# Finer waits at three seams of a spectral and dense layer stack: the returned components by quarters, the last tile's rows by halves of tokens, three late stores from another queue

One core of a Trainium2 chip. The metric is the device time of one execution in microseconds (us), lower is better.

## The reference

A stack of four residual layers on `x` of 1 x 2048 tokens x 1024 channels, bf16: spectral layer A, dense layer B, A again, B again.

```python
def _A_ref(x, w_r, w_i):                     # S = 2048 tokens, D = 1024
    X = jnp.fft.rfft2(x.astype(jnp.float32), axes=(-2, -1))
    X = X * (w_r + 1j * w_i)
    return jnp.fft.irfft2(X, s=(S, D), axes=(-2, -1)).astype(jnp.bfloat16)

def _B_ref(x, w1, b1, w2):                   # F = 3584
    h = jnp.einsum("bsd,df->bsf", x, w1) + b1
    sp = jnp.log1p(jnp.exp(-jnp.abs(h))) + jnp.where(h > 0, h, 0)
    return jnp.einsum("bsf,fd->bsd", h * jnp.tanh(sp), w2)

x = x + _A_ref(_layernorm(x), w_r, w_i)
x = x + _B_ref(_layernorm(x), w1, b1, w2)
x = x + _A_ref(_layernorm(x), w_r, w_i)
x = x + _B_ref(_layernorm(x), w1, b1, w2)
```

## The kernel before

The Fourier transforms are products with tables on TensorE. Layer A works in 8 groups `g` of 16 components. Near its end each group's tile `u` is written to DRAM and read back with components on the partitions (the "turn"), into one tile `UT`; the last products (`i4`) read it, four groups of 32 products over `l` (called dl, 0 to 127), and VectorE adds each group to `x`. From layer B to the next layer A the normalised tokens must change layout too: tile `j` (128 tokens) goes to DRAM and back into `XR`, and the last tile, 15, is copied inside SBUF row by row (`xr_direct`). A `Res` is what waits are made of: `reads` waits for its writers, `parts` writes a part of it without waiting for the other writers. Cuts are marked.

```python
    def xn_store(self, j, b):
        b.unread = False
        self.dma(self.pool, self.xn_d[j], b.ap, "xw" + b.res.name[2:], reads=[b.res], writes=[self.r_xnd[j]])

    def open_xr(self):
        self.XR = self.alloc("XR", self.o["XR"], [P, P])
        self.XR.res.begin()
        self.r_xr = [self.XR.res] * 4

    def xr_load(self, j):
        self.dma(self.pool, self.XR.ap[row_of(j, 0):row_of(j, 7) + 1:4, :, :], self.xn_d[j].rearrange(...), f"xl{j % 4}",
                 reads=[self.r_xnd[j]], parts=[self.XR.res])

    def xr_direct(self, j, b):
        for h in range(8):                            # 32 KB each, into one partition
            prog = (self.sp, self.act, self.pool)[h % 3]
            self.dma(prog, self.XR.ap[row_of(j, h):row_of(j, h) + 1, :, :], b.ap[:, h * P:(h + 1) * P], "xd" + prog.name,
                     reads=[b.res], parts=[self.XR.res])
    # ... (s1: 16 groups of 8 products, group j reads self.r_xr[j // 4])

        def u_turn(g, half):
            u = U[g % 3]
            if g == 7:                                # last group: stored in two halves of its components
                h = slice(8 * half, 8 * half + 8)
                if half == 0:
                    self.r_ud[g].begin()
                self.dma(act, self.u_d[g][:, h, :], u.ap[:, h, :], f"uwh{half}", reads=[u.res], parts=[self.r_ud[g]])
            elif half:
                self.dma(sp, self.u_d[g], u.ap, f"uw{g % 3}", reads=[u.res], writes=[self.r_ud[g]])
            if g and (half == 0) == (g == 7):
                u_back(g - 1)
            if g == 7 and half:
                u_back(7)

        def u_back(g):                                # 16 rows: g, g + 8, ...
            for i, prog in enumerate((sp, act) if g == 7 else (sp,)):
                l = slice(64 * i, 64 * i + 64) if g == 7 else slice(0, P)
                self.dma(prog, self.UT.ap[g:P:8, l, :], self.u_d[g][l].rearrange("l r n -> r l n"), f"u{prog.name}{g % 3}",
                         reads=[self.r_ud[g]], parts=[self.UT.res])
    # ... (i4: self.group(fns, reads=[self.UT.res, self.r_mt], writes=rb))
```

## Time and profile before

| | before |
|---|---|
| time | 1050.99 us median of 4 (1050.31 to 1052.5); the profiled run 1051.39, its trace spans 1049.6 |
| TensorE busy | 91% of the span |
| granted TensorE clock, mean | 0.966 |
| waits of TensorE at the three seams | 11.9, 12.0 and 11.9 us |
| DMA moved | 107 MB, 102 GB/s mean |

The three waits, 3.4% of the span, are the subject. In a wait line such as `PE PS L588 <- DMA ARENA<-ARENA: 12.0, 1, 12.0` the engine before the arrow stood for what is behind it: 12.0 us in total, once, 12.0 at most. In all views PE is TensorE, DVE VectorE, ACT ScalarE, POOL GpSimd and SP SyncE; in a DMA row each digit is the busy share of the 16 DMA engines in one slice, in tenths. Line numbers are those of each kernel's own file, so `L588` before is `L594` after, and `L901` is `L919`. The lines of before stand in the prediction.

### The profile page before, as it was taken

To read this page: it belongs to the slowest core of one execution; us is meant where nothing else is said; L and a number is where in the kernel's file an instruction comes from. 1 tells how busy PE (TensorE), PEld (TensorE's weight loads), DVE (VectorE), ACT (ScalarE), POOL (GpSimd) and SP (SyncE) were. 2 spreads that over 40 slices of the span, in tenths; PEclk is the share of its full clock that TensorE was granted. 3 is DMA by queue.
4 is the path that set the end of the run, shared out by engine and by line. 5 is a ranking of instruction groups with operands and counts; after the bars stand their busy time and mean duration, and the time that the engine had idled before them with its cause. 6 is when DMAs were issued, how large, how long until landed. Compare 5 with 4: busy or idle time off the path is not lost.

```text
span 1049.6 us, 14096 instructions
## 1 busy us (share of the span) xinstructions
PE 952.5 (91%) x5944; PEld 511.7 (49%) x6033; DVE 350.8 (33%) x776; ACT 336.5 (32%) x503; POOL 71.0 (7%) x114
## 2 busy tenths in 40 slices
PE   0799489999999999999959967999999999999998
PEld 0567465444444444444427746644444444444443
DVE  6898562531343100043326856426011100000111
ACT  6898263331000333300008844533300013340000
POOL 3242000000000000002421200000000000000000
PEclk9699789999999999999989987999999999999999
DMA  9779812464111221001941784145611112200000
GB/s 281 176 257 281 221 44 91 151 200 134 50 52 37 69 64 39 1 21 71 178 83 44 222 210 131 42 151 166 209 25 45 45 63 81 61 1 11 21 21 31
DMA packets 152718, 107.01 MB, mean 102 GB/s; under 512 B 74288, under 2 KB 131888, under 8 KB 152656
## 3 DMA queue, kind: packets, MB, share of 16 engines
q1 hardware_dynamic: 139936, 75.99, 25.4%
q0 software_dynamic: 9632, 28.45, 9.5%
q10 hardware_dynamic: 3088, 1.67, 0.6%
q8 instruction: 48, 0.79, 0.3%
q14 instruction: 14, 0.11, 0.0%
HBM read 80.85 MB, written 20.71 MB: 97 GB/s over the span
## 4 chain that ended last, share of the span: by engine, by line
PE 80%; DVE 9%; ACT 6%; DMA 3%; issue 1%; SPq 0%; ACTq 0%; DVEq 0%
PE PS L994 37%; PE PS L976 37%; DVE BN L459 2%; ACT ARENA L721 2%; PE PS L669 2%; DVE XS L915 1%; DVE ARENA L573 1%; DVE ARENA L790 1%; DMA u_scratch<-ARENA 1%; DMA ARENA<-u_scratch 1%; ACT ARENA L704 1%; DVE ARENA L951 1%; DVE ARENA L596 1%; PE PS L901 1%; ACT ARENA L792 1%
## 5 line engine op out<-in xcount | busy, mean ns | idle before, releaser
L976 PE MATMUL PS<-ARENA 128*128 128x512 bf16 (+1 forms) x1946 | 390.6, 360 | 10.3 <-DVE ARENA L951 7.2
L994 PE MATMUL PS<-ARENA 128*128 128x512 bf16 x1756 | 385.5, 379 | 1.9
L980 ACT ACTIVATE ARENA<-PS,B 128x512 bf16<-128x512 f32 (+1 forms) x248 | 159.8, 646 | 438.7 <-PE PS L976 438.7
L976 PEld LDWEIGHTS PS<-ARENA 128*128 128x128 bf16 x1984 | 194.2, 99 | 201.8 <-DVE ARENA L951 8.7
L994 PEld LDWEIGHTS PS<-ARENA 128*128 128x128 bf16 x1792 | 175.3, 98 | 211.5
L999 DVE TENSOR_TENSOR XS<-PS,XS 128x512 bf16<-128x512 f32 x64 | 44.3, 692 | 537.9 <-PE PS L994 537.9
L459 DVE BATCH_NORM_STATS2 BN<-XS 128x6 f32<-128x512 bf16 x104 | 67.2, 675 | 7.5 <-DMA XS<-in_A_x_dram 6.3
L915 DVE TENSOR_TENSOR XS<-PS,XS 128x512 bf16<-128x512 f32 (+1 forms) x40 | 29.1, 790 | 82.0 <-PE PS L901 82.0
L901 PE MATMUL PS<-MT,ARENA 128*128 128x32 bf16 (+1 forms) x768 | 24.5, 187 | 27.2 <-DMA ARENA<-u_scratch 23.8
L901 PEld LDWEIGHTS PS<-MT,ARENA 128*128 128x128 bf16 x768 | 23.0, 100 | 30.7 <-issue 24.7
L440 ACT ACTIVATE ARENA<-XS 128x1024 bf16<-128x1024 bf16 x24 | 25.3, 1055 | 36.4 <-DVE XS L915 31.5
L721 ACT ACTIVATE ARENA<-PS 128x1024 bf16<-128x1024 f32 x32 | 33.9, 1060 | 8.5 <-PE PS L717 8.5
L669 PE MATMUL PS<-FD,ARENA 128*128 128x256 bf16 (+1 forms) x256 | 33.6, 278 | 2.9 <-ACT ARENA L594 1.2
L750 ACT ACTIVATE ARENA<-PS 128x1024 bf16<-128x1024 f32 x32 | 33.9, 1061 | 3.7 <-PE PS L743 3.7
L249 POOL DMA_DIRECT2D xn_scratch<-ARENA x15 | 8.2, 550 | 390.7 <-DVE ARENA L498 390.7
L431 ACT ACTIVATE RS<-MV,EPS 128x1 f32<-128x1 f32 (+1 forms) x7 | 2.0, 292 | 98.5 <-DVE MV L462 96.2
L743 PE MATMUL PS<-ARENA 128*128 128x256 bf16 x256 | 33.2, 273 | 0.1
L743 PEld LDWEIGHTS PS<-ARENA 128*128 128x128 bf16 x256 | 24.5, 98 | 10.0 <-DVE ARENA L732 1.2
L725 DVE TENSOR_TENSOR ARENA<-ARENA 128x1024 bf16<-128x1024 bf16 x32 | 22.0, 687 | 21.9 <-ACT ARENA L721 21.9
L669 PEld LDWEIGHTS PS<-FD,ARENA 128*128 128x128 bf16 x256 | 24.5, 100 | 8.4 <-DVE ARENA L596 2.8
L764 PE MATMUL PS<-ARENA,BD 128*128 128x256 bf16 x192 | 25.9, 273 | 1.3 <-DVE ARENA L790 1.0
L498 DVE TENSOR_SCALAR ARENA<-XS,MV,RS 128x1024 bf16<-128x1024 bf16 x48 | 25.0, 543 | 1.0
(70 smaller groups left out, 503.8 us busy)
## 6 DMA issues: line engine op xcount, KB each, us to landing
ARENA<-in_B_w_dram SPq DMA_DIRECT2D x56, 512.0 KB, 3.9
ARENA<-in_B_w_dram SPq DMA_DIRECT2D x56, 256.0 KB, 4.2
u_scratch<-ARENA SPq DMA_DIRECT2D x14, 512.0 KB, 3.6
ARENA<-u_scratch SPq DMA_DIRECT2D x14, 512.0 KB, 5.7
XS<-in_A_x_dram SPq DMA_DIRECT2D x4, 1024.0 KB, 8.6
w_scratch<-ARENA POOLq DMA_DIRECT2D x8, 512.0 KB, 5.6
ARENA<-w_scratch POOLq DMA_DIRECT2D x8, 512.0 KB, 5.2
out_dram<-XS SPq DMA_DIRECT2D x16, 256.0 KB, 2.2
```

The source lines that it names most:

```text
L459: self.op(self.dve, lambda e: e.bn_stats(self.BN[:, j, 6 * h:6 * h + 6], self.XS[:, j, 512 * h:512 * h + 512]), reads=[self.r_xs[j]], part ...
L669: fns.append(lambda e: e.matmul(dst, at(r), FD[:, t:t + n], start=start, stop=stop))
L721: self.op(act, lambda e: e.activation(x.ap.rearrange("p a b -> p (a b)"), ps, ACT.Copy, scale=SIG), reads=banks, writes=[x.res])
L743: fns.append(lambda e, c=c, part=part: e.matmul(ps[:, c * 256:(c + 1) * 256], yk.ap[:, part, c * P:(c + 1) * P], t[:, (128, 0)[part]:(384, ...
L750: self.op(act, lambda e: e.activation(v.ap[:, :, i, :], src, ACT.Copy), reads=banks, parts=[v.res])
L764: fns.append(lambda e, dst=dst, part=part, c=c: e.matmul(dst, BD[:, c:c + P], mov(kd, part), start=(part == 0), stop=(part == 1)))
L901: fns.append(lambda e, l=l: e.matmul(ps[:, w * l:w * l + w], self.UT.ap[:, u0 + l, :], self.MT[:, 8 * lo:8 * lo + w], start=True, stop=True))
L915: self.op(self.dve, lambda e: e.tensor_tensor(xs, src, xs, ALU.add), reads=rb, parts=self.r_xs[lo:lo + nb])
L976: fns.append(lambda e, db=db, bank=bank, fl=fl: e.matmul(PS[:, bank, 0:w], wb.ap[:, db, fl * P:(fl + 1) * P], x.ap[:, db, tok], start=(db ...
L980: self.op(act, lambda e, bank=bank, ft=ft: e.activation(at.ap[:, ft, tok], PS[:, bank, 0:w], ACT.Mish, bias=self.B1[:, ft:ft + 1]), reads= ...
L994: fns.append(lambda e, i=i, ft=ft: e.matmul(PS[:, bank, :], at.ap[:, ft, t * P:(t + 1) * P], W2[ft].ap[:, h * 512:(h + 1) * 512], start=(i ...
L999: self.op(dve, lambda e: e.tensor_tensor(xs, PS[:, bank, :], xs, ALU.add), reads=[self.r_bank[bank]], writes=[self.r_xs[j]])
```

## The change

The intent: a product waits only for the part that it reads. The last group comes back in pieces (half 0 of its rows once half 0 is stored, half 1 by quarters of dl), `UT` has four resources, one for each group of products; `XR` has two, one for each half of the last tile's tokens; tiles 12 to 14 are stored by SyncE, so that GpSimd's queue only loads: before, tile 14, normalised by 527.88, was stored only at 534.90, behind tile 13's load. Arithmetic and its order on TensorE, VectorE and ScalarE are the same.

```diff
     def xn_store(self, j, b):
-        self.dma(self.pool, self.xn_d[j], b.ap, "xw" + b.res.name[2:], ...)
+        prog = self.sp if j >= 12 else self.pool
+        self.dma(prog, self.xn_d[j], b.ap, f"xw{prog.name}{b.res.name[2:]}", ...)
     def open_xr(self):
-        self.XR.res.begin()
-        self.r_xr = [self.XR.res] * 4
+        halves = self.sub_res(self.XR, "xrh", 2, self.o["XR"], P * P * 2)
+        # ... begin() on both
+        self.r_xr = [halves[0], halves[0], halves[1], halves[1]]
     def xr_direct(self, j, b):
-        for h in range(8):
-            prog = (self.sp, self.act, self.pool)[h % 3]
-            self.dma(prog, self.XR.ap[row_of(j, h):row_of(j, h) + 1, :, :], b.ap[:, h * P:(h + 1) * P], ...)
+        for i in range(16):
+            half, h = i // 8, i % 8
+            n = slice(64 * half, 64 * half + 64)
+            prog = (self.sp, self.act, self.pool)[i % 3]
+            self.dma(prog, self.XR.ap[row_of(j, h):row_of(j, h) + 1, n, :], b.ap[n, h * P:(h + 1) * P], ...,
+                     reads=[b.res], parts=[self.r_xr[2 * half]])
         def u_turn(g, half):
             # ... (g == 7: each half's store has its own resource r_ud7[half]; after the second one:)
+                if half:
+                    u_last()
+        def u_last():
+            def back(prog, half, q, n):
+                l = slice(32 * q, 32 * q + 32 * n)
+                self.dma(prog, self.UT.ap[7 + 64 * half:P if half else 64:8, l, :],       # 8 rows
+                         self.u_d[7][l, 8 * half:8 * half + 8, :].rearrange("l r n -> r l n"),
+                         f"ul{half}{q}", reads=[self.r_ud7[half]], parts=self.r_ut[q:q + n])
+            back(sp, 0, 0, 2)
+            back(sp, 0, 2, 2)
+            for q in range(4):
+                back((act, sp)[q % 2], 1, q, 1)
     # i4
-        self.group(fns, reads=[self.UT.res, self.r_mt], writes=rb)
+        self.group(fns, reads=self.r_ut[u0 // 32:(u0 + n - 1) // 32 + 1] + [self.r_mt], writes=rb)
```

More of the change, by code (lines that the diff above doesn't have):

```diff
@@ L341, in build @@
             self.r_ud = [Res(f"ud{i}") for i in range(8)]
+            self.r_ud7 = [Res(f"udh{i}") for i in range(2)]
             self.r_wd = [Res(f"wd{i}") for i in range(8)]
@@ L504, in xn_store @@
         b.unread = False
-        self.dma(self.pool, self.xn_d[j], b.ap, "xw" + b.res.name[2:], reads=[b.res], writes=[self.r_xnd[j]])
+        prog = self.sp if j >= 12 else self.pool
+        self.dma(prog, self.xn_d[j], b.ap, f"xw{prog.name}{b.res.name[2:]}", reads=[b.res], writes=[self.r_xnd[j]])
     def open_xr(self):
         self.XR = self.alloc("XR", self.o["XR"], [P, P])
-        self.XR.res.begin()
-        self.r_xr = [self.XR.res] * 4
+        halves = self.sub_res(self.XR, "xrh", 2, self.o["XR"], P * P * 2)
+        for r in halves:
+            r.begin()
+        self.r_xr = [halves[0], halves[0], halves[1], halves[1]]
     def xr_load(self, j):
         self.dma(self.pool, self.XR.ap[row_of(j, 0):row_of(j, 7) + 1:4, :, :], self.xn_d[j].rearrange("n (h l) -> h n l", l=P), f"xl{j % 4}",
-                 reads=[self.r_xnd[j]], parts=[self.XR.res])
+                 reads=[self.r_xnd[j]], parts=self.r_xr[1:3])
     def xr_direct(self, j, b):
         b.unread = False
-        for h in range(8):
-            prog = (self.sp, self.act, self.pool)[h % 3]
-            self.dma(prog, self.XR.ap[row_of(j, h):row_of(j, h) + 1, :, :], b.ap[:, h * P:(h + 1) * P], "xd" + prog.name,
-                     reads=[b.res], parts=[self.XR.res])
+        for i in range(16):
+            half, h = i // 8, i % 8
+            n = slice(64 * half, 64 * half + 64)
+            prog = (self.sp, self.act, self.pool)[i % 3]
+            self.dma(prog, self.XR.ap[row_of(j, h):row_of(j, h) + 1, n, :], b.ap[n, h * P:(h + 1) * P], f"xd{half}{prog.name}",
+                     reads=[b.res], parts=[self.r_xr[2 * half]])
     def pair(self):
@@ L799, in u_turn @@
                 if half == 0:
-                    self.r_ud[g].begin()
-                self.dma(act, self.u_d[g][:, h, :], u.ap[:, h, :], f"uwh{half}", reads=[u.res], parts=[self.r_ud[g]])
+                    u_back(6)
+                self.dma(act, self.u_d[g][:, h, :], u.ap[:, h, :], f"uwh{half}", reads=[u.res], writes=[self.r_ud7[half]])
+                if half:
+                    u_last()
             elif half:
                 self.dma(sp, self.u_d[g], u.ap, f"uw{g % 3}", reads=[u.res], writes=[self.r_ud[g]])
-            if g and (half == 0) == (g == 7):
-                u_back(g - 1)
-            if g == 7 and half:
-                u_back(7)
+                if g:
+                    u_back(g - 1)
         def u_back(g):
-            for i, prog in enumerate((sp, act) if g == 7 else (sp,)):
-                l = slice(64 * i, 64 * i + 64) if g == 7 else slice(0, P)
-                self.dma(prog, self.UT.ap[g:P:8, l, :], self.u_d[g][l].rearrange("l r n -> r l n"), f"u{prog.name}{g % 3}",
-                         reads=[self.r_ud[g]], parts=[self.UT.res])
+            self.dma(sp, self.UT.ap[g:P:8, :, :], self.u_d[g].rearrange("l r n -> r l n"), f"usp{g % 3}",
+                     reads=[self.r_ud[g]], parts=self.r_ut)
+        def u_last():
+            def back(prog, half, q, n):
+                l = slice(32 * q, 32 * q + 32 * n)
+                self.dma(prog, self.UT.ap[7 + 64 * half:P if half else 64:8, l, :], self.u_d[7][l, 8 * half:8 * half + 8, :].rearrange("l r n -> r l n"),
+                         f"ul{half}{q}", reads=[self.r_ud7[half]], parts=self.r_ut[q:q + n])
[3 more added lines that the diff above has]
+                back((act, sp)[q % 2], 1, q, 1)
         self.s1(li)
@@ L822, in layer_A @@
         self.UT = self.alloc("UT", o["UT"], [P, P])
-        self.UT.res.begin()
+        self.r_ut = self.sub_res(self.UT, "ut", 4, o["UT"], P * P * 2)
+        for r in self.r_ut:
+            r.begin()
         for step in range(8 + 3):
@@ L849, in layer_A @@
         while self.w1_next < 28 * li + 6:
-            self.load_w1(after=[self.UT.res])
+            self.load_w1(after=self.r_ut)
     def load_wr(self, wr, g):
```

## The prediction

> **What bounds the kernel now.** I read the page's slices first, then the chain of waits in order of time, then the waits where TensorE stops, then the DMA and queue views of those places. TensorE's row:
>
> ```profile
> PE   0799489999999999999959967999999999999998
> ```
>
> A slice is 26.2 us. TensorE is full nearly everywhere; after the start there are three thin places, slices 5, 21 and 24 to 25, around 110 to 130, 537 to 549 and 620 to 640 us. They are the seams: the end of the first spectral layer, the change from the first dense layer to the second spectral layer, and the end of that one. The chain of waits names what stands there:
>
> ```profile
> 113.11 4.96 DMA u_scratch<-ARENA
> 118.15 4.75 DMA ARENA<-u_scratch
> 123.14 1.03 PE PS L901 x32
> 124.19 4.63 DVE XS L915 x4
> ...
> 541.26 7.34 DMA ARENA<-ARENA
> 549.05 6.48 PE PS L588 x64
> ...
> 622.15 5.01 DMA u_scratch<-ARENA
> 627.23 4.77 DMA ARENA<-u_scratch
> 632.14 1.03 PE PS L901 x32
> ```
>
> Everything else in the chain is untouched by the change. TensorE's waits there, in total, times and longest:
>
> ```profile
> PE PS L901 <- DMA ARENA<-u_scratch: 23.8, 2, 11.9
> PE PS L588 <- DMA ARENA<-ARENA: 12.0, 1, 12.0
> ```
>
> So 35.8 us, 3.4% of the span, is the most that finer waits could ever touch; most of it is real transfer and stays.
>
> At seams one and three (call them the turn seams) the last group's components go to DRAM in two halves and come back transposed, and the turned tile UT is one resource: the first of four groups of 32 products waits for all of it. At the middle seam the last tile's rows are copied within SBUF, and the first of 16 product groups waits for all rows of all tiles. GpSimd's queue just before it:
>
> ```profile
> 527.39 1.13 POOL L249 DMA_DIRECT2D ARENA<-xn_scratch  x1 [6.37 <-DMA xn_scratch<-ARENA]
> 528.52 0.58 POOL L249 DMA_DIRECT2D xn_scratch<-ARENA  x1
> 533.81 1.09 POOL L249 DMA_DIRECT2D ARENA<-xn_scratch  x1 [4.71 <-DMA xn_scratch<-ARENA]
> 534.90 0.58 POOL L249 DMA_DIRECT2D xn_scratch<-ARENA  x1
> 540.00 1.09 POOL L249 DMA_DIRECT2D ARENA<-xn_scratch  x1 [4.52 <-DMA xn_scratch<-ARENA]
> 541.08 1.13 POOL L249 DMA_DIRECT2D ARENA<-ARENA  x2
> ```
>
> Stores and loads of tiles 12, 13, 14 alternate on one in-order queue, each load waiting for its store. VectorE had normalised tile 14 by 527.88, yet its store left at 534.90 and its load at 540.00, the very moment the last tile's rows (tile 15, ready at 539.97) set out. In the trace's semaphore increments that load completes at 547.50 and the direct copies at 548.24 (ScalarE's), 548.42 (GpSimd's) and 548.59 (SyncE's). The first copy of SyncE and of ScalarE, which moved before that load's packets began at 541.75, have all 16 counts by 544.2 and 543.7 at the latest: 3.7 to 4.2 us after issue. The later ones took over 7.
>
> The DMA engines through the first turn seam, 108 to 123 us in 40 slices:
>
> ```profile
> DMA  0079998999999999999999999999996999998100
> GB/s 0 0 328 404 262 229 180 237 290 290 287 221 287 317 437 388 258 288 332 326 362 281 318 414 337 287 287 285 242 154 117 255 261 245 223 203 128 29 0 0
> ```
>
> They are full from 109 to 122: seven half-megabyte transfers (three stores, four copies back) are queued behind each other. This seam is mostly bandwidth and only at its end a wait.
>
> [...] issues cost 0.5 to 0.6 us, and the two last halves back, issued together at 118.13 and 118.15, landed 0.9 us apart. [...] Before, a copy back has 16 rows; after, the last group's has 8[...]. No copy of that shape from SyncE stands in this trace. [...] the trace moves such a copy's 512 KB in about 2.3 us, 228 GB/s[...]. [...] granted clock 0.64 from 111 to 123.1, and half speed until 554.8 after the middle seam.
>
> **The change, part by part.** Instructions on TensorE, VectorE and ScalarE's compute are the same in number and order; only DMA issues and waits change.
>
> *Middle seam, stores from SyncE.* Tiles 12 to 14 are stored by SyncE, which has nothing else to do there. Tile 14's store then leaves at 527.9 and, at the 2.2 to 2.7 us of an undisturbed store, lands by about 530.5; its load leaves then and is in by about 535 (the loads of 12 and 13 took 5.2 to 5.5 us from issue). The 256 KB that now share the engines with the direct copies are gone 5 us before them.
>
> *Middle seam, halves of tokens.* 8 copies of 32 KB become 16 of 16 KB, half 0 first, dealt round to three queues. SyncE issues numbers 0, 3, 6 of half 0, ScalarE 1, 4, 7, GpSimd 2, 5. Three issues at 0.57: the last leaves at 540.0 + 2 x 0.57 = 541.15. An undisturbed first copy had its first 8 counts after 2.5 us and the other 8 about 1.05 us later; half the bytes into one partition should halve that second term: 2.5 + 0.5 = 3.0. So half 0 is complete at about 544.15, and with the 0.46 us seen between 548.59 and 549.05, TensorE starts at 544.6: **4.4 us earlier**. Half 1 is needed 8 groups later; 64 products took 6.48 us, so at 551. Its last issue leaves by 543.0 and lands by 547: hidden.
>
> *Turn seams.* Transfers, in order: the last copies of groups 5 and 6, then group 7. Group 6's copy back is issued at 114.87 and its packets run 117.0 to 119.2; group 7's before ran 119.3 to 122.1 and completed at 121.97 and 122.89. After: half 0 of group 7 (256 KB) may be issued once its store has landed at 116.70 instead of 118.07, but it queues behind group 6 until 119.2, so this gives only the small dip in the row above. From there, 2048 pieces of 256 B on 8 engines. The trace spends 14 ns per piece and engine when full (about 282 pieces in 0.25 us on 16), so 8 engines move 144 GB/s: 512 KB take 3.6 us, to about 122.8, plus 0.75 for completion, 123.6. That is 0.7 later than now for the last quarter. Quarter 0 however needs half 0's first 128 KB, half 1's 64 KB and what interleaves, about 256 KB: 1.8 us, complete by about 121.7. TensorE then starts at about 121.9 against 123.14. VectorE's four additions of 1.16 us are the chain behind it; the second needs quarter 1, about 448 KB into the queue, 122.3 + 0.75 = 123.1, and so waits some 0.4 us; quarters 2 and 3 are then in time. Gain 1.2 - 0.4 = **0.8 us at each seam**, instead of the 2 to 3 that "by quarters" suggests. The weight loads that follow move 0.7 later; the first needs 5 us and its products come at 134, so that is free.
>
> Sum: 4.4 + 2 x 0.8 = 6.0 us; 1050.8 - 6.0 = **1044.8 us**, 0.6%.
>
> **The rivals.** *Eight engines bite harder.* [...] VectorE stalls again, and both turn seams give 0 or lose up to 1. For it: the engines are full there[...]. [...] Time: about 1047 to 1048.5. *The copies keep 16 engines.* Then the last quarter lands as now and quarter 0 about 2 us earlier; 1.8 us each: 1042.8. *The direct copies are slow of themselves.* Twice as many descriptor issues and single-partition targets; if the 7 us were theirs and not tile 14's load, half 0 gains only its share, 2 to 3 us: 1046.5. Against it: the first ones were done in 4 us. [...]
>
> **Range and chances.** The middle seam's 4.4 may be 3 to 5.3, each turn seam -1 to 1.8, clock and run spread +-1.5. Eight in ten: 1041.8 to 1048.4. Two per cent is 21 us, more than half of all three waits together: within 2% is near certain, 0.98, and 0.01 each side.
>
> **What would show each step.** Wait of the first spectral products on the direct copies 7.5 us instead of 12.0, tile 14's load issued near 530 from GpSimd, no second wait between product groups 8 and 9. At the turn seams a first wait near 10.7 instead of 11.9, smaller waits of the second group of products, DMA busy shares near half[...] after the turn of group 6, last quarter at about 123.6. The prediction is wrong if the middle wait stays above 9, if half 1 is waited for, or if the turn seams end later than 128.8 (the last addition now).

That eight rows come over eight engines was assumed, and on it rest the 144 GB/s and the 0.8. Of the rival "eight engines bite harder" the rate behind it is cut, so its outcome stands as an estimate of mine; a rival about TensorE's clock is cut whole, and the clock's share of the +-1.5 was not shown (the four runs of before spread over 1050.31 to 1052.5).

## The result, and the profile after

1047.49 us median of 4 (1046.63 to 1048.44), before 1050.99; ratio 0.9965, 95% interval 0.9948 to 0.9982. A ratio here is the mean time of one kernel's fast runs over that of the other's fast runs of the same rounds, so not quite the ratio of the medians. Repeated in later rounds the change had 1047.66 against 1051.01, ratio 0.9968. All ratios in this document lie within 2% of 1; differences are told here by their intervals. The gain is some 3.5 us of the 6.0 that I predicted; 1047.49 lies within the range.

The chain of waits of the changed kernel, in order of time (start, length, what):

```profile
113.41 4.98 DMA u_scratch<-ARENA
118.41 5.22 DMA ARENA<-u_scratch
123.86 1.03 PE PS L919 x32
124.92 4.63 DVE XS L933 x4
...
542.08 2.30 DMA ARENA<-ARENA
544.73 3.58 PE PS L594 x32
...
621.94 5.26 DMA ARENA<-u_scratch
627.34 1.03 PE PS L919 x32
```

and its waits over the whole span:

```profile
PE PS L919 <- DMA ARENA<-u_scratch: 24.7, 2, 12.4
PE PS L594 <- DMA ARENA<-ARENA: 7.1, 1, 7.1
```

The middle seam's wait fell from 12.0 to 7.1 us, as predicted (7.5). The turn seams did not fall at all: 24.7 in place of 23.8, and the copy back takes 5.22 and 5.26 in the chain in place of 4.75 and 4.77. The four additions behind the first turn follow in 4.63 us as before: VectorE never waits for a later quarter, because the first comes so late.

To see where the 4.76 us between the two traces' spans (1049.58 and 1044.82) lie, I cut both at events that they share: the last evacuation of each layer A (the last copy of products out of PSUM before the turn), the first product with `w2`, and the end of the last tile's normalisation. Times from the traces' instruction records:

| stretch | before | after | gain |
|---|---|---|---|
| start to last evacuation, first layer A | 113.08 | 113.38 | -0.30 |
| from there to the first product with `w2` (first turn seam) | 133.55 | 133.85 | -0.30 |
| of it, evacuation to first product of the turn | 10.03 | 10.45 | -0.42 |
| last tile normalised to last evacuation (middle seam, second A) | 82.16 | 76.28 | +5.88 |
| of it, to the first product | 9.06 | 4.14 | +4.92 |
| second turn seam, to the first product with `w2` | 133.38 | 134.31 | -0.93 |
| of it, evacuation to first product of the turn | 9.99 | 10.46 | -0.47 |
| the other two stretches | 587.41 | 587.00 | +0.41 |

What lies beyond the waits goes with the stretches in which TensorE had half its clock. After the middle seam the half clock ended at 548.43 in place of 554.81, against a start only 4.3 us earlier on that clock; in the second turn seam it now lasts 4.9 us into the dense products, from 639.15 to 644.01, before 2.9 (644.11 to 646.97). That this need not be the work of the turn's new copies shows in the middle-only run below: its turn is untouched, its first product comes after 10.08 us, and still that seam takes 134.26 us, 0.88 more than before.

GpSimd's queue before the middle seam in the changed kernel (timeline):

```profile
524.73 1.06 POOL L249 DMA_DIRECT2D ARENA<-xn_scratch  x1 [2.70 <-DMA xn_scratch<-ARENA]
533.51 1.06 POOL L249 DMA_DIRECT2D ARENA<-xn_scratch  x1 [7.72 <-DMA xn_scratch<-ARENA]
540.85 2.70 POOL L249 DMA_DIRECT2D ARENA<-ARENA  x5 [6.28 <-DVE ARENA L499]
543.55 0.57 POOL L249 DMA_DIRECT2D ARENA<-c_ft  x1
```

Tile 14's load left at 533.51 and had landed at 537.97, before the direct copies set out at 540.59. Note the last line: a table load stands right behind the direct copies in this queue. Before, it stood there too, at 542.20. It becomes important below.

The DMA engines from 117 to 127 us, 40 slices of 0.25 us; first before, then after:

```profile
DMA  9999999995999999999410000000356899999999
GB/s 362 283 293 289 287 282 253 199 141 88 212 257 262 253 244 227 207 206 157 64 16 0 0 0 0 0 0 0 70 98 172 256 377 322 330 326 328 338 332 344
```

```profile
DMA  9999999999996666666666666676313000000013
GB/s 428 365 304 283 289 291 282 252 219 191 178 138 108 115 112 108 103 103 99 102 103 114 141 144 122 107 108 101 58 23 66 0 0 0 0 0 0 2 37 80
```

Before, the last half megabyte moves at 200 to 260 GB/s; after, the row of nines turns into sixes and the rate sinks to 100 to 115 GB/s for over 3 us. The semaphore of each of the six copies has one early increment (1.1 to 1.8 us after its issue) and eight when the data lands, where a copy of 16 rows has 16. I read this as eight engines; the trace does not name them. And the copies of half 1 hardly ran beside half 0: ScalarE issued half 1's quarter 0 at 118.41, its first packets stand at 121.75, behind all but some 70 of half 0's 1024, and it landed at 123.62. That copy is what the first product waited for.

### The profile page after: what moved, and what is told of

It reads as the page before. It is cut to its first block, busy times and chain, and to the rows that moved or that the text cites. A ratio compares the mean times of both kernels' runs of the same rounds, so it can differ in the third digit from the quotient of the medians.

```text
span 1044.8 us, 14118 instructions
## 1 busy us (share of the span) xinstructions
PE 951.7 (91%) x5944; PEld 510.5 (49%) x6033; DVE 350.9 (34%) x776; ACT 336.4 (32%) x503; POOL 71.1 (7%) x114
## 4 chain that ended last, share of the span: by engine, by line
PE 80%; DVE 9%; ACT 6%; DMA 3%; issue 1%; ACTq 0%; DVEq 0%
PE PS L994 37%; PE PS L1012 37%; DVE BN L460 2%; ACT ARENA L727 2%; PE PS L675 2%; DVE XS L933 1%; DVE ARENA L579 1%; DVE ARENA L796 1%; DMA ARENA<-u_scratch 1%; DMA u_scratch<-ARENA 1%; ACT ARENA L710 1%; DVE ARENA L969 1%; DVE ARENA L602 1%; PE PS L919 1%; ACT ARENA L798 1%
## 5 line engine op out<-in xcount | busy, mean ns | idle before, releaser
L919 PE MATMUL PS<-MT,ARENA 128*128 128x32 bf16 (+1 forms) x768 | 24.3, 187 | 27.4 <-DMA ARENA<-u_scratch 24.7
```

The costliest lines, as they stand in the source:

```text
L919: fns.append(lambda e, l=l: e.matmul(ps[:, w * l:w * l + w], self.UT.ap[:, u0 + l, :], self.MT[:, 8 * lo:8 * lo + w], start=True, stop=True))
```

## The experiments

Ten kernels with parts of the change or variants of it, and the change once more, all correct; 5 runs each (one had 6). "Start" is the time from the last tile's normalisation (or, at the turn seams, from the last evacuation) to the first product, from the one trace of each kernel.

**The middle seam alone.** The hunks on `xn_store`, `open_xr`, `xr_load` and `xr_direct` only.

> The change at the middle seam alone (stores of tiles 12 to 14 from SyncE, the last tile's rows by halves of tokens); the turn of the components as before. Theory A (the middle seam gains 4.9 us as the two traces show, 9.1 us from the normalised tile to TensorE's first product down to 4.2; the narrow copies at the turn seams take about 0.5 us back at each): 1046.1, ratio 0.9953, so faster than the whole change by about 1 us. Rival B (the turn parts are neutral[...]): the same as the whole change, 1047.5.

1046.43 us against 1050.51, ratio 0.9962 (0.9949 to 0.9974); middle start 4.15, turn starts 10.06 and 10.08. The middle seam carries the whole gain: 4.0 us. By the ratios it is 0.3 to 0.6 us better than the change (0.9965 and 0.9968), well inside the intervals: the times do not tell theory A from rival B.

**The turn seams alone.** The other hunks only.

> The change at the two turn seams alone (group 7 back by halves of rows and quarters of dl); the middle seam as before. Theory A: slower than before by about 1 us, 1052, with the first product after the turn 0.4 to 0.6 us later than before counted from the landing of the last store. Rival B: 1051, equal to before. My prediction on record would have it faster by 1.6.

1049.94 against 1050.51, ratio 1.0001 (0.9988 to 1.0013): my predicted gain of 1.6 us lies outside the interval, theory A's loss of about 1 us does not. The trace has both signs: the first turn starts at 10.49, 0.45 later than before's 10.03, the second at 9.06, 0.9 earlier. In the change's two traces all four starts are late (10.45, 10.46, 10.38, 10.41). Why the one was early is left open; the turn parts are worth nothing that these runs show, within 1.3 us.

**Two copies of eight rows, nothing else.** This isolates the narrow shape: as many copies and bytes as before.

```diff
-            for i, prog in enumerate((sp, act)):          # 16 rows, 64 of dl each
-                self.dma(prog, self.UT.ap[7:P:8, l, :], self.u_d[7][l]..., reads=[self.r_ud[7]], ...)
+            for half, prog in enumerate((sp, act)):       # 8 rows, all of dl; each after its own half's store
+                self.dma(prog, self.UT.ap[7 + 64 * half:P if half else 64:8, :, :],
+                         self.u_d[7][:, 8 * half:8 * half + 8, :]..., reads=[self.r_ud7[half]], parts=self.r_ut)
```

> Before, with the last group's copy back as two copies of 8 rows over all of dl (each after its own half's store), instead of two copies of 16 rows over half of dl: the same number of copies and bytes, 8 rows in place of 16, the turned tile waited for as a whole. Theory A (8 rows are carried by 8 of the 16 engines, 3.6 us instead of 2.8 for the packets): the last copy lands 1.5 to 2.5 us later after the last store than before's 4.8 us, each turn seam longer by that, 1054 to 1056. Rival C (the later landing in the changed kernel comes from six copies in place of two, by their issues and completions): as before or up to 1 us better per seam, since half 0 may go earlier: 1049 to 1051.

1054.13 against 1050.51, ratio 1.004 (1.0027 to 1.0053). The last copies land 6.83 and 7.10 us after the last store (before 4.8), starts 12.05 and 12.23. The number of copies is not the cause; the shape is, together with the later start of the second half. The DMA row of this run from 117 to 127:

```profile
DMA  9999999999999997666666666666666520000000
GB/s 285 292 310 395 401 339 293 291 288 292 270 251 203 189 164 122 110 112 108 109 103 102 100 102 103 134 143 142 115 108 103 78 39 2 0 0 0 0 0 0
```

For most of it about 105 GB/s. My estimate for eight engines was 144, from the fast stretch of a full copy. Full copies have a slow one too. Before, group 7's second copy, 16 rows from ScalarE, moved alone from 121.0 to 121.5 (all 405 packets are of its queue, q10):

```profile
DMA packets 405, 0.10 MB, mean 206 GB/s; under 512 B 405, under 2 KB 405, under 8 KB 405
```

Half of these 206 is 103: eight rows have half the increments (8 for 16 in the changed kernel), by my reading half the engines, and the slow rate of a full copy (206 GB/s are 20 ns for 256 B on each of 16 engines) would be halved with them. The fast stretch: group 6's moved at 287 from 117.5 to 118.5, 14 ns. And in the row above half 1, alone by then, moves at 134 to 143 for 0.75 us before it falls to 105.

**The same two copies, leaving together.** Both wait for both stores, so that the two halves of the partitions can be written at once.

```diff
-                         reads=[self.r_ud7[half]], parts=self.r_ut)
+                         reads=self.r_ud7, parts=self.r_ut)
```

> As the eight-row experiment, but both copies (rows of half 0 from SyncE, of half 1 from ScalarE) wait for both stores and so leave together. [...] Theory F (one half alone moves at 105 GB/s[...]; 8 engines as such can move 144 GB/s): if the two interleave, 512 KB take about 3.6 us and the last lands 5.6 to 6.0 us after the last store, between before's 4.8 and the 6.8 to 7.1 of the staggered form: 1052 to 1052.5. Rival G (a copy on 8 engines has 105 GB/s[...]): last landing about 6.8 or later, 1054.

```profile
DMA  9999999999996445655666666666400000001339
GB/s 308 348 409 365 311 288 289 289 275 258 203 145 95 90 117 136 141 135 133 137 131 145 145 144 142 144 144 145 103 0 0 0 0 0 0 0 43 72 94 283
```

131 to 145 GB/s, steady from 120.75 on, last landing 6.1 us after the store, 1051.9 against 1050.16, ratio 1.002 (1.0007 to 1.0032). Rate and landing are near what theory F expected, and rival G is out: copies of eight rows are not held to 105. But theory F is not shown by this. The packets by queue (packets, MB, share of the 16 engines' time; q1 is SyncE's copy, half 0, q10 ScalarE's, half 1) from 120.5 to 121.5, from 122 to 123 and from 123.25 to 124:

```profile
q1 hardware_dynamic: 517, 0.13, 57.2%
```

```profile
q1 hardware_dynamic: 277, 0.07, 31.5%
q10 hardware_dynamic: 276, 0.07, 31.3%
```

```profile
q10 hardware_dynamic: 424, 0.11, 63.6%
```

At the start and at the end only one half was in motion, and it moved at 132 and 145 GB/s all the same. So one half alone is not held to 105 from the first packet on; a limit that binds only after some time would fit both runs, and so would the start: here the copies followed engines that had nearly run dry (90 GB/s at 120.25), in the staggered form half 0 followed group 6's slow last packets without a gap. What sets the 105 is open. Shown is that the narrow copies cost time in both orders, 3.6 us staggered and 1.7 together.

**Four quarters of 16 rows.** The change, with the six copies replaced.

```diff
-            back(sp, 0, 0, 2)
-            back(sp, 0, 2, 2)
-            for q in range(4):
-                back((act, sp)[q % 2], 1, q, 1)
+            for q in range(4):
+                l = slice(32 * q, 32 * q + 32)
+                self.dma((act, sp)[q % 2], self.UT.ap[7:P:8, l, :], self.u_d[7][l]..., reads=self.r_ud7, parts=self.r_ut[q:q + 1])
```

> The whole change, but the last group comes back as four copies of 16 rows by 32 of dl, each after both halves' stores, instead of six copies of 8 rows. Theory A: 16 engines per copy, quarter 0 lands about 1.5 to 2 us earlier than before (3.0 to 3.4 us after the last store's landing instead of 4.8), the last at about before's time; VectorE's additions start that much earlier and each turn seam gains about 1.6: 1051 - 4.9 - 3.2 = 1042.9. Rival C (number of copies): no better than the change, 1047.

1044.88 against 1050.51, ratio 0.9948 (0.9935 to 0.9962). Quarter 0 lands 3.84 us after the last store instead of 4.82, starts 9.06 and 8.83. Gain about 1 us per seam, not the 1.6 expected: quarter 0 went out from ScalarE and landed after SyncE's quarter 1 (122.53 and 121.89).

**The stores alone.** Only the hunk on `xn_store`.

> Before, with only the stores of tiles 12 to 14 issued by SyncE. Theory D (the middle seam's gain is made of two parts that need each other: the load of tile 14 out of the way, and half the bytes before the first product): the load of tile 14 leaves near 533 as in the changed kernel; the eight copies of 32 KB run undisturbed, the last issued 1.2 us after the tile and done about 4.0 us later, so TensorE starts about 5.6 us after the tile's normalisation instead of 7.3 to 9.1 in the four traces of the old form; gain 2.5, 1048.2. Rival E (halves of tokens are what matters): 1050 or more, start over 7 us after the tile.

1050.79 against 1050.16, ratio 1.0003 (0.9989 to 1.0017), start 7.24. Theory D failed here. Tile 14's load was out of the way (landed at 537.54, the tile normalised at 541.0), but the table load was issued at 542.43, 1.4 us after the first direct copy where in the full change it is 3.0, and its packets of 4608 B held the engines from 543.7 to 545.7 at 485 to 1122 ns each (175 to 535 in the changed kernel); the third copies of SyncE and ScalarE stood behind them.

**The halves alone.** Only `open_xr`, `xr_load`, `xr_direct`.

> Before, with only the last tile's rows by halves of tokens. Theory D: GpSimd's two copies of half 0 still stand behind tile 14's load in its queue, and the load's packets share the engines with the others: half 0 is complete 5.5 to 7 us after the tile, TensorE starts there; gain 1 to 2, 1049 to 1050. Rival E: start at 4.2 us as in the whole change, gain 4, 1046.5.

1049.95 against 1050.16, ratio 0.9999 (0.9987 to 1.0012), start 6.60. The start lies in the range that theory D expected, but the four traces with the old middle part start between 6.58 and 9.06, so it is no gain by itself, and the time shows none. Each part alone is worth nothing that the clock shows; together they are worth 4.0.

**The stores alone, table load held back.**

```diff
     def load_tabs(self, g):
-        self.dma(self.pool, b.ap, self.con["FT"][g], f"ft{g % 3}", writes=[b.res])
+        self.dma(self.pool, b.ap, self.con["FT"][g], f"ft{g % 3}", writes=[b.res],
+                 reads=[self.Y.res] if self.li and g == 2 else [])
```

> As the stores-only kernel, and the 192 KB table load that GpSimd issues right behind its direct copies now waits until the spectral products of the seam are done. My theory D failed on stores alone: TensorE still started 7.24 us after the tile. Theory H (the table load took the place of tile 14's load beside the direct copies: its 4608-byte packets took 730 to 980 ns each from 543.5 to 545.5, and the third copy of each queue stood in that time): with it out of the way TensorE starts 5.0 to 6.0 us after the tile. Theory I (eight rows of 32 KB into single partitions are slow of themselves): it starts at 6.8 us or later. The time follows by 1.5 to 2.5 us if H, so 1048.3; the table is needed more than 10 us later.

Waits of TensorE at this seam, in the stores-only kernel, then here:

```profile
PE PS L589 <- DMA ARENA<-ARENA: 10.1, 1, 10.1
```

```profile
PE PS L589 <- DMA ARENA<-ARENA: 9.2, 1, 9.2
```

1048.98 against 1051.01, ratio 0.9984 (0.9972 to 0.9997), start 6.34: between the two theories. By one trace each the table load is worth 0.9 us, less than the 2.5 by which the old form's own starts differ, so this share is a hint; the timed gain over before is some 1.7 us. With no table and no load of tile 14 beside them the eight copies of 32 KB still take 2.2 us longer than half 0's eight copies of 16 KB (4.14). So the size counts, and the company probably.

**Quarters of groups 5, 6 and 7, first quarters first.** A candidate. Every first quarter is fetched before any later one, so the DMA engines no longer carry bytes that the first products do not need.

```diff
-                if g: u_back(g - 1)                   # groups 5 and 6 whole
+                # quarter 0 of group 5 where group 5 went, of group 6 where group 6 went; after the last store:
+            for g, q in ((5, 1), (6, 1), (7, 0), (7, 1)): u_quarter(sp, g, q)
+            # quarters 2 and 3 of groups 5, 6, 7 alternately from ScalarE and SyncE, after both stores
```

> Candidate: the middle seam as changed; at the turn seams groups 5, 6 and 7 all come back by quarters of dl with 16 rows each, quarter 0 of all three first, quarters 2 and 3 only after the last stores have landed. Theory: the DMA engines are full from 109 to 122 in this seam, with bytes that the first products do not need; with quarter 0 first, the last stores land about 2 us earlier (115.7 to 116.5) and quarter 0 is complete at about 118.5 to 119.5 on the clock of the kernel before, 3.5 to 4.3 us before its 122.9; later quarters arrive about 1.7 us apart against 1.16 us per addition and cost up to 1 us. Gain 3 per turn seam plus 4 in the middle: 1040.5. Rival: the many issues (10 to 12 copies at 0.55 to 1.2 us) and the 128 KB size cost as much as the order brings: about 1045, as with four quarters of the last group alone.

```profile
117.28 3.64 DMA ARENA<-u_scratch
121.16 1.03 PE PS L927 x32
122.21 4.68 DVE XS L941 x4
```

1042.29 against 1050.16, ratio 0.9927 (0.9914 to 0.9939): the best version, faster than both kernels. The last store lands 3.3 us after issue instead of 5.0, the first product comes 7.54 and 7.46 us after the last evacuation instead of 10.0, and the additions stay at VectorE's own pace. Expected 1040.5; quarter 0 of group 7 landed at 120.92, later than the 118.5 to 119.5 that I had put.

**The same from one queue, in order of need.**

```diff
+            for g, q in ((5, 1), (7, 0), (6, 1), (7, 1), (5, 2), (6, 2), (7, 2), (5, 3), (6, 3), (7, 3)): u_quarter(sp, g, q)
```

> Candidate: as the early-quarters kernel, all quarters from SyncE in order of need (5.1, 7.0, 6.1, 7.1, then the second and third quarters). In the early-quarters kernel the copy that TensorE waited for (group 7, quarter 0) was issued 0.4 us after the last store had landed and stood behind or beside 3 to 4 others: 7.5 us from the last evacuation to the first product. With it next in line it should land 2.8 to 3.2 us after the store, first product at 6.7: 0.8 us per seam, 1040.7 or so. Rival: the queue's 0.6 us per issue for ten copies delays quarters 2 and 3 and VectorE waits for them: as the early-quarters kernel, 1042.3, or up to 1 us slower.

1044.17 against 1051.01, ratio 0.9938 (0.9925 to 0.9952). TensorE's timeline in the first turn seam:

```profile
119.53 1.01 PE L920 MATMUL PS<-MT,ARENA 128*128 128x32 bf16 x32 [8.03 <-DMA ARENA<-u_scratch]
120.90 1.02 PE L920 MATMUL PS<-MT,ARENA 128*128 128x32 bf16 x32 [0.36 <-DMA ARENA<-u_scratch]
124.04 1.01 PE L920 MATMUL PS<-MT,ARENA 128*128 128x32 bf16 x32 [2.13 <-DMA ARENA<-u_scratch]
125.56 3.57 PE L920 MATMUL PS<-MT,ARENA 128*128 128x32 bf16 x128 [0.50 <-DMA ARENA<-u_scratch]
```

The first product came 1.4 us earlier than with two queues, as expected and more, and more than all of it was lost again, in waits for later quarters of which the third's, 2.13 us, is the longest: the rival. A first wait made shorter is worth only what the next parts can follow.

**The change again.**

> The changed kernel unaltered, on the same chip and in the same rounds as the candidate, to size the change once more: 1046.5 to 1047.5; its middle seam starts 4.1 to 4.7 us after the tile (in the two traces with both parts 4.14 and 4.15, in the candidate 4.65), its turn seams 10 to 10.5 us after the last evacuation, 9 in a lucky one.

1047.66 against 1051.01, ratio 0.9968 (0.9956 to 0.998); starts 10.38, 4.11, 10.41.

## Why the prediction was right or wrong

Its time, 1044.8, was 2.7 us low and within its range, which was wide enough to hold both its own account of the turn seams and the rival's. By its steps:

- **What bounds the kernel, and the cap of 35.8 us.** Right. Outside the seams the two traces differ by -0.30 and +0.41 us.
- **Middle seam, 4.4 us.** Right in size: 4.92 between the two traces, 4.0 by the timed run of that part alone. My one trace of before had a slow seam: four traces with its middle part untouched start at 9.06, 8.42, 7.28 and 6.58, while all six with the changed one lie between 4.11 and 4.65. Half 1 is hidden, as predicted. That 4.4 came so near is partly luck: it is reckoned from the slowest of the four old starts (their mean is 7.8), and the new start, put at 4.6, came 0.5 earlier. And the reason was too simple. I put the late copies down to tile 14's load alone; with that load gone the table load took its place (stores alone: 7.24), and with that gone too the full-size copies still take 6.34. What I listed as a rival, copies slow of themselves, is a part of the truth. The changed kernel escapes the table load because its five GpSimd copies stand before it in the queue, which I had not reckoned as part of the gain.
- **Tile 14's load near 530.** Wrong without harm: 533.51. SyncE's store took 4.7 us (528.50 to 533.23), because, it seems, the loads of tiles 12 and 13 were still moving (they landed at 530.93 and 532.55); I had taken 2.2 to 2.7 from undisturbed stores.
- **Eight engines for eight rows.** Right as far as the trace shows it: eight increments with the data, where 16 rows have 16.
- **Turn seams, 0.8 us each.** Wrong, and this is the failed step: "Quarter 0 however needs half 0's first 128 KB, half 1's 64 KB and what interleaves, about 256 KB: 1.8 us, complete by about 121.7." Almost nothing interleaved. Half 1's first packets came at 121.75, behind nearly all of half 0, and half 0 moved at about 105 GB/s, not 144, so quarter 0 was complete at 123.62. The 144 rests on 14 ns per piece and engine, the fast stretch of a full copy; the same trace of before has 20 ns in group 7's own copy, and at that rate eight engines would move 103. The 228 GB/s that the prediction gives for a full copy is likewise a mean, of a stretch at 287 and a slow rest. The prediction's first rival named the outcome, "give 0 or lose up to 1"; what holds half 0 to 105 is not shown. Measured: -0.42 and -0.47 in the pair of traces, 0 within 1.3 us by the timed run. I gave that rival too little weight, because I took it that two queues would feed the two halves at once; the trace of the change shows that they were fed one after the other (half 1's first packets 3.3 us after its issue; why is open), while in the together run the two queues took even turns (277 and 276 packets from 122 to 123).
- **Its own signs of being wrong.** One came: the first turn's last addition ended at 129.55, later than the 128.8 that it had named; the middle wait (7.1) and half 1 (no wait) passed.
- **The wait for quarter 1, 0.4 us.** It did not occur: with quarter 0 at 123.62, quarters 1 to 3 (124.25, 124.79, 125.35) were each in time.
- **The sum.** 4.4 + 1.6 against 4.0 + 0: the missing term is the turn seams'. Beyond the first products, the stretches with half clock in them gained 1.0 us after the middle seam (5.88 against 4.92) and lost 0.5 in the second turn (0.93 against 0.47) in the profiled run; over runs this is not told from their spread (1046.63 to 1048.44).

## What to carry to other kernels

Here a finer wait paid only where the transfers came in the order in which they were waited for and the finer pieces still moved at about the rate of whole ones: cutting along rows left 8 increments of 16 and some 100 to 145 GB/s, cutting along the free dimension 177 to 256 GB/s while the four quarters moved (before: 200 to 260). Where the DMA engines are full up to the wait, look first at the bytes ahead of the awaited ones; moving those back (first quarters of all groups first) brought 7.7 us in all, splitting the last transfer into quarters 5.5, both with the middle seam's 4.0. And a collision removed may only make room for the next transfer in the queue, so try two parts of a change both alone and together.
